# Giving the feature maps and the normalized rows' copies to ScalarE behind the slot's exponential

## The chip, the cores and the metric

The kernel runs on one core of one Trainium2 chip. The metric is the device time of one execution in microseconds (us). A core has TensorE (matmuls; PE in the profile, with PEld for its weight loads), VectorE (DVE), ScalarE (ACT), GpSimd (POOL) and SyncE (SP, which here issues most transfers). Each engine works through its own list of instructions in order, and semaphores make one engine wait for another.

## What is computed

The reference is one transformer block over 2048 rows of width 512, modulated by a condition vector `c`: a layer norm, an attention with a compressive memory (32 heads of width 16, four segments of 512 rows), an output projection, a second layer norm, and a bilinear feed-forward layer of width 1376. What matters here is the attention of one segment:

```python
phi = lambda t: jnp.where(t > 0, t + 1.0, jnp.exp(t))
for s in range(N):                       # 4 segments
    logits = jnp.einsum("bhqd,bhkd->bhqk", qs, ks) * scale + mask
    a_dot = jnp.einsum("bhqk,bhkd->bhqd", _softmax(logits, axis=-1), vs)
    pq = phi(qs)
    a_mem = (pq @ M) / (pq @ z + 1e-6)   # memory of the earlier segments
    o = g * a_mem + (1.0 - g) * a_dot
    pk = phi(ks)
    M = M + pk^T @ vs; z = z + sum(pk)
```

So every segment but the last needs the feature map `phi` of its keys, and every segment but the first that of its queries. The kernel computes `phi(t)` as min(exp(t), 1) + relu(t): a Relu and an Exp on ScalarE and one step on VectorE that joins them.

## The kernel before, in words

The heads are worked in 4 groups (`g`) of 8, for 4 segments (`s`), in halves of 4 heads: 32 units `v`. The main loop (lines 1149 to 1199) takes each unit through five slots. In each slot TensorE's work is given out in this order: the first half of the query-side scores of a later unit (`q_half(u, i, 0)`, PSUM tile `lq0`), whose row maxima VectorE finds in place (tiles `q` and `nm` of the profile); in slot 1 the product of probabilities and values (`av_step`, tile `tb`); in slot 4 the transposes of a finished unit (`t_step`, tile `tr`, read by VectorE as `rd` and `orow`); filler work (`fill`); the second half of the scores (`q_half(u, i, 1)`, tile `lq1`); and the key-side scores (`k_step`, tile `k`), whose exponential ScalarE takes as one operation of 128x1024 (tile `pt`, line 335). `lq0`, `lq1` and `k` have one buffer each: the next matmul into one of them waits until VectorE, or ScalarE, has read it.

The filler `fill_a` (line 974) computes the projections of the next groups: `a_kq` (line 799) runs twelve matmuls for `kps` or `qps` in four steps, copies the result to SBUF (`kf`, `qf`, line 819), takes a first bfloat16 part of it on ScalarE (line 823), and where a feature map is needed gives out `feature` (Relu into `rl`, Exp into `ph`, line 847, each ordered behind the latest exponential given out so far, `lastex`). One step later `rest` (line 826) makes the other two parts, and the list `later` takes up `feature2`, VectorE's joining step. The lists work thus: `flush` gives out all of `later`, after the first half of the scores in each slot and whenever a filler step asks for a PSUM bank (`bank`); `behind` holds closures that the main loop gives out at the end of a slot, behind `k_step` (line 1192); `after_n` goes over to `later` in slot 2; `settle` empties all three, and `a_mem` (the memory step that multiplies `ph` with the memory, tiles `mp`, `up`, `mz`) calls it before it reads `ph`.

In the loop VectorE's instructions are chained in the order in which the program gives them out (`vec.eng = CV`, line 1147). TensorE's are chained too. ScalarE's and GpSimd's are not: the scheduler of the language orders them by when they are ready in its own timeline, and the program's order is the tie-break.

Before the change only two feature maps go through `behind` (`held`, line 854): the keys of groups 2 and 3 of segment 0. In `ln` (line 172) the normalized rows of segments 1 to 3 are transposed, scaled and shifted on ScalarE (`ahf`, line 223), and split at once into a first part on ScalarE (`ahH`, line 233) and a rest on GpSimd (`ahL`, line 234). Slots are called below by the instant of their k matmuls or of their exponential.

Of the kernel before, what the change touches and what calls it, by code (L numbers as in the profile page):

```python
# [8 lines left out]
F32 = mybir.dt.float32  # L9
F32R = mybir.dt.float32r  # L10
BF = mybir.dt.bfloat16
AF = mybir.ActivationFunctionType
# [13 lines left out]
NOSYNC = mybir.DependencyInfo(mybir.DependencyClass.NoSync, mybir.DependencyReason.DATA)  # L26
# [31 lines left out]
def tile_kernel(ctx, tc, x, wq, wk_, wv, wo, beta, w_gate, w_up, w_down, c, w_mod, out):  # L58
    nc = tc.nc
# [19 lines left out]
    def pin(i):  # L79

        if last_pe[0] is not None:
            tc.add_manual_dep(i.ins, last_pe[0].ins.name, NOSYNC, reason="order")
# [4 lines left out]
    def TP(*a):  # L87
        return pe(nc.tensor.transpose(*a))

    CV, CA = Chain(tc, nc.vector), Chain(tc, nc.scalar)  # L90
    vec, act = Switch(nc.vector), Switch(nc.scalar)
# [15 lines left out]
    behind, lastex, after_n, now = [], [None], [], [0]  # L107
# [19 lines left out]
    def bank(name, dt=F32, shape=(P, 512), small=False):  # L127

        flush()
        rest_of()  # L130
        nbank[0] += 1
        tag = btag[nbank[0] % len(btag)]
        if tag == "ms":
            if not small:
                nlast[0] ^= 1
            tag = f"ms{nlast[0] ^ int(small)}"
        return pst(shape, tag, name, dt)
# [34 lines left out]
    def ln(pool, hpool, xt, s, sc, sh, pfx, hb, fast):  # L172

        first = pfx == "a" and s == 0
        V, A = (CV, CA) if first else (vec, act)
        mv = pool.tile([P, 4, 2], F32, tag="mv", name=f"{pfx}mv{s}", bufs=2)
        for t in range(4):
            st = pool.tile([P, 6], F32, tag="st", name=f"{pfx}st{s}_{t}", bufs=2)
            i = V.bn_stats(st, xt[t])
            if not first:  # L180
                pin(i)
            V.bn_aggr(mv[:, t, :], st)
            if not first:
                yield 0.0
        sd = pool.tile([P, 4], F32, tag="sd", name=f"{pfx}sd{s}", bufs=2)
        A.activation(sd, mv[:, :, 1], AF.Ln, bias=epst[:, 0:1])
        y = pool.tile([P, 4], F32, tag="y", name=f"{pfx}y{s}", bufs=2)
        A.activation(y, sd, AF.Exp, scale=-0.5)
        a = pool.tile([P, 4], F32, tag="ya", name=f"{pfx}ya{s}", bufs=2)
        b = pool.tile([P, 4], F32, tag="yb", name=f"{pfx}yb{s}", bufs=2)  # L190
        eng = CV if first else nc.gpsimd
        eng.tensor_mul(a, y, y)
        if first:
            CV.scalar_tensor_tensor(b, mv[:, :, 1], EPS, a, op0=ALU.add, op1=ALU.mult)
        else:
            eng.tensor_scalar(b, mv[:, :, 1], 1.0, EPS, op0=ALU.mult, op1=ALU.add)
            eng.tensor_mul(b, b, a)
        eng.tensor_scalar(b, b, -0.5, 1.5, op0=ALU.mult, op1=ALU.add)
        eng.tensor_mul(y, y, b)
        yield 0.0  # L200
        tps = [bank(f"{pfx}tp{s}_{d}") for d in range(KT)] if first else []
        for t in range(4):
            i = V.tensor_scalar(xt[t], xt[t], mv[:, t, 0:1], y[:, t:t + 1],
                                op0=ALU.subtract, op1=ALU.mult)
            if not first:
                pin(i)
                yield 0.0
            for d, ps in enumerate(tps):
                TP(ps[:, t * P:(t + 1) * P], xt[t][:, d * P:(d + 1) * P], ident)
        if first:  # L210
            yield 0.0
        hH, hL = [], []
        if first:
            hcur[0] = hH, hL
        for d in range(KT):
            if first:
                ps = tps[d]
            else:
                ps = bank(f"{pfx}tp{s}_{d}", small=pfx == "c" and s == 0)
                for t in range(4):  # L220
                    TP(ps[:, t * P:(t + 1) * P], xt[t][:, d * P:(d + 1) * P], ident)
            h = pool.tile([P, L], F32, tag="hf", name=f"{pfx}hf{s}_{d}", bufs=hb[2])
            A.activation(h, ps, AF.Identity, scale=sc[:, d:d + 1], bias=sh[:, d:d + 1])
            hi = hpool.tile([P, L], F32R, tag=hb[0].format(d), name=f"{pfx}hH{s}_{d}", bufs=hb[1])
            lo = hpool.tile([P, L], F32R, tag=hb[0].format(4 + d), name=f"{pfx}hL{s}_{d}", bufs=hb[1])
            if fast:
                if d % 2:
                    A.activation(hi, h, AF.Copy)
                else:
                    V.tensor_copy(hi, h)  # L230
                V.tensor_sub(lo, h, hi.bitcast(F32))
            else:
                act.activation(hi, h, AF.Copy)
                nc.gpsimd.tensor_sub(lo, h, hi.bitcast(F32))
            hH.append(hi)
            hL.append(lo)
            yield 0.45
            if pfx == "a" and not first and d % 2 == 1:
                yield False
        return hH, hL  # L240
# [558 lines left out]
    def a_kq(s, g, nm):  # L799

        hH, hL = hcur[0]
        ph = phs.setdefault((s, g), {})
        if True:
            dst = kd if nm == "k" else qd
            ps = bank(f"{nm}ps{s}_{g}")
            n = 0
            three = ((wH, hH), (wH, hL), (wL, hH)) if s == 0 and g < 2 else ((wH, hH), (wL, hH), (wH, hL))
            terms = [(k, *ab) for k in range(KT) for ab in three]
            if s == 0 and g == 1:
                terms.sort(key=lambda t: t[1] is wL)  # L810
            for k, a, b in terms:
                MM(ps, a[nm, g][:, k, :], b[k], start=n == 0, stop=n == 11)
                n += 1
                if n in (3, 6, 9):
                    yield 0.68
            f = pa.tile([P, L], F32, tag="f", name=f"{nm}f{s}_{g}", bufs=2)
            fast = s == 0 and g == 0
            A, V = (CA, CV) if fast else (act, nc.gpsimd)
            A.activation(f, ps, AF.Copy)
            q3 = pa.tile([P, 3, L], BF, tag="q3", name=f"{nm}3_{s}_{g}", bufs=2)  # L820
            r = pa.tile([P, L], F32, tag="qr", name=f"{nm}r_{s}_{g}", bufs=2)
            i0, i1, i2 = (0, 1, 2) if nm == "k" else (2, 1, 0)
            A.activation(q3[:, i0, :], f, AF.Copy)
            V.tensor_sub(r, f, q3[:, i0, :])

            def rest():
                (CV.tensor_copy if fast else act.copy)(q3[:, i1, :], r)
                V.tensor_sub(q3[:, i2, :], r, q3[:, i1, :])
                nc.sync.dma_start(dst[s][g].rearrange("r p t -> p r t"), q3)

            if fast:
                rest()
            phi = (nm == "k" and s < NSEG - 1) or (nm == "q" and s > 0)
            if phi:
                if fast:
                    yield 0.0
                if nm == "q" and g > 0:
                    yield from drain()
                e = pa.tile([P, L], F32, tag="ph", name=f"ph{nm}{s}_{g}", bufs=3)
                if behind:  # L840
                    settle()
                rl = pa.tile([P, L], F32, tag="rl", name=f"rl{nm}{s}_{g}", bufs=1)
                ph[nm] = e

                def feature():
                    for a, fn in ((rl, AF.Relu), (e, AF.Exp)):
                        i = (CA if fast else act).activation(a, f, fn)
                        if lastex[0] is not None:
                            tc.add_manual_dep(i.ins, lastex[0].ins.name, NOSYNC, reason="order")

                def feature2():
                    pin((CV if fast else vec).scalar_tensor_tensor(e, e, 1.0, rl, op0=ALU.min, op1=ALU.add))

                held = s == 0 and g > 1
                if held:
                    behind.append(lambda: (feature(), (after_n if now[0] == 0 else later).append(feature2)))
                else:
                    feature()
            yield 0.68
            if not fast:  # L860
                rest()
            if phi and not held:
                later.append(feature2)
                if fast:
                    flush()
        nkq[s, g] = nkq.get((s, g), 0) + 1
        if nkq[s, g] == 2:
            done.add((s, g))
# [105 lines left out]
    def fill_a():  # L974
# [5 lines left out]
        for s in range(NSEG):  # L980
            if s > 0:
                hcur[0] = yield from lns
                if s < 3:
                    r = load_mod(2 * s)
            for g in range(2 if s == 0 else 0, NG):
# [163 lines left out]
    for v in range(-2, NQ + 1):  # L1149
        rate[0] = 5.5  # L1150
        on, prev = 0 <= v < NQ, 0 <= v - 1 < NQ
        for slot in range(5):
            i = (slot + 3) % 5
# [450 lines left out]
    for n in range(NU):  # L1604
        p, nm, i = units[n]
# [69 lines left out]
```

## Time and profile before

| | |
|---|---|
| median of 3 runs | 861.65 us (860.18 to 862.78) |
| the profiled execution | 862.23 us, of it 860.5 us from the first instruction to the last |
| VectorE busy | 643.1 us, 75% |
| ScalarE busy | 499.1 us, 58% |
| GpSimd busy | 275.8 us, 32% |

The page gives for each engine its busy time and share of the span. A row of the timeline gives an instruction's start and duration in us, its engine and line, what it writes from what, and in square brackets how long its engine stood idle before it and what ended that wait. Rows of one kind that follow each other are merged (x4). The attention loop runs from about 41 us to about 490 us; the rest is the feed-forward layer.

### The profile page before, as it was taken

What the parts mean: (1) busy time and instruction counts of PE and PEld (TensorE: products, weight loads), DVE (VectorE), ACT (ScalarE), POOL (GpSimd) and SP (SyncE); (2) the same over time, 40 slices, a digit from 0 to 9 for tenths busy, and PEclk for the clock granted to TensorE, in tenths of its full rate; (3) what the DMA queues carried; (4) which work ended last, traced back from release to release, by engine and by line L of the source; (5) the groups of instructions that cost most, each with busy time, mean ns of one, the idle gap of its engine ahead of it and who ended that gap; (6) DMA issues with size and microseconds to landing.
All of it is one profiled execution on the core that took longest, in us unless ns stands there. A gap on an engine that the chain in (4) does not pass through costs nothing.

```text
span 860.5 us, 14421 instructions
## 1 busy us (share of the span) xinstructions
PE 839.1 (98%) x4982; PEld 599.1 (70%) x4982; DVE 643.1 (75%) x1796; ACT 499.1 (58%) x759; POOL 275.8 (32%) x423
## 2 busy tenths in 40 slices
PE   9989999999999999999999999999999999999998
PEld 6756655566665666666665677788888778888886
DVE  6897766887778877687889358989987855446554
ACT  4758766777677786677545626343535546455230
POOL 2756526566545673675424610000000000000000
PEclk9999999999999999999999999999999999999999
DMA  8655433655527463458575447578561576335102
GB/s 269 148 151 158 121 102 88 183 136 167 142 82 197 113 177 100 122 155 245 144 239 166 137 159 247 207 239 324 197 226 50 214 263 212 143 135 183 34 17 98
DMA packets 83929, 139.57 MB, mean 162 GB/s; under 512 B 12721, under 2 KB 46769, under 8 KB 83857
## 3 DMA queue, kind: packets, MB, share of 16 engines
q1 hardware_dynamic: 83568, 138.52, 51.9%
q8 instruction: 39, 0.64, 0.3%
q14 instruction: 34, 0.27, 0.1%
q10 hardware_dynamic: 288, 0.15, 0.1%
HBM read 89.87 MB, written 48.50 MB: 161 GB/s over the span
## 4 chain that ended last, share of the span: by engine, by line
PE 84%; ACT 7%; DVE 6%; issue 1%; POOL 0%; DMA 0%; DVEq 0%; ACTq 0%
PE acc L1351 14%; PE tb L85 8%; PE Xg L1282 7%; PE Xu L1282 7%; PE k L85 6%; PE q L85 6%; PE wops L85 5%; PE vps L85 5%; PE kps L85 4%; PE Yu L1282 4%; PE Yg L1282 4%; DVE q L39 3%; PE qps L85 3%; ACT pt L335 2%; PE Zg L1282 1%; PE Zu L1282 1%
## 5 line engine op out<-in xcount | busy, mean ns | idle before, releaser
L39 DVE CUSTOM_DVE_ANT_0 q<-q,cmask 128x384 f32<-128x384 f32 (+3 forms) x512 | 247.6, 504 | 71.3 <-PE q L85 63.6
L335 ACT ACTIVATE pt<-k 128x1024 f32<-128x1024 f32 x160 | 163.9, 1024 | 76.9 <-PE k L85 75.0
L341 POOL TENSOR_SCALAR_AFFINE_SELECT pt<-pt 128x256 f32<-128x256 f32 (+1 forms) x224 | 98.6, 454 | 152.8 <-ACT pt L335 150.2
L85 PE MATMUL q<-kst,qst 96*128 96x384 bf16 (+3 forms) x512 | 123.0, 302 | 7.6 <-DVE nm L39 6.0
L85 PE MATMUL k<-qst,kst 98*128 98x384 bf16 (+3 forms) x512 | 95.9, 299 | 5.7 <-ACT pt L335 5.2
L1359 DVE TENSOR_TENSOR xa<-xa,acc 128x512 f32<-128x512 f32 x95 | 64.8, 684 | 39.8 <-PE acc L1351 39.3
L85 PEld LDWEIGHTS <-qst 96*128 96x128 bf16 x512 | 44.2, 98 | 59.2 <-issue 44.1
L85 PE MATMUL tb<-pt,v 128*32 128x512 f32 (+3 forms) x1024 | 77.1, 442 | 0.0
L39 DVE DVE_READ_ACCUMULATOR2_ANT nm<- 128x1 f32 x512 | 71.9, 140 | 0.0
L85 PEld LDWEIGHTS <-kst 98*128 98x128 bf16 x512 | 44.5, 97 | 30.2 <-issue 15.2
L1351 PE MATMUL acc<-dH,mH 128*128 128x512 f32 (+1 forms) x152 | 60.3, 397 | 0.0
L1351 PE MATMUL acc<-dL,mH 128*128 128x512 f32 (+1 forms) x152 | 60.1, 395 | 0.0
L1351 PE MATMUL acc<-dH,mL 128*128 128x512 f32 (+1 forms) x152 | 60.0, 394 | 0.0
L85 PEld LDWEIGHTS tb<-pt,v 128*32 128x32 f32 x1024 | 28.8, 110 | 40.1 <-issue 37.3
L367 ACT ACTIVATE tsb<-tb 128x512 f32<-128x512 f32 x32 | 19.1, 596 | 32.5 <-PE tb L85 32.5
L1351 PEld LDWEIGHTS acc<-dL,mH 128*128 128x128 f32 (+1 forms) x152 | 28.6, 188 | 7.0
L1351 PEld LDWEIGHTS acc<-dH,mL 128*128 128x128 f32 (+1 forms) x152 | 28.5, 188 | 7.1 <-DVE mL L1302 0.3
L1351 PEld LDWEIGHTS acc<-dH,mH 128*128 128x128 f32 (+1 forms) x152 | 28.5, 188 | 6.7
L85 PE MATMUL kps<-ahH,wkH 128*128 128x512 f32 x64 | 29.5, 461 | 0.0
L85 PE MATMUL wops<-woH,oH 128*128 128x512 f32 x64 | 28.2, 441 | 0.8 <-ACT oH L530 0.7
L85 PE MATMUL qps<-ahH,wqH 128*128 128x512 f32 x64 | 28.7, 448 | 0.0
L85 PE MATMUL vps<-wvH,ahH 128*128 128x512 f32 x64 | 28.3, 443 | 0.0
(399 smaller groups left out, 2018.4 us busy)
## 6 DMA issues: line engine op xcount, KB each, us to landing
wm<-in_w_mod_dram SPq DMA_DIRECT2D x24, 256.0 KB, 4.9
kd<-k SPq DMA_DIRECT2D x16, 384.0 KB, 2.5
qd<-q SPq DMA_DIRECT2D x16, 384.0 KB, 3.6
kst<-kd SPq DMA_DIRECT2D x32, 192.0 KB, 3.3
qst<-qd SPq DMA_DIRECT2D x32, 192.0 KB, 3.7
x<-in_x_dram SPq DMA_DIRECT2D x16, 256.0 KB, 4.9
kst<-kd SPq DMA_DIRECT2D x32, 128.0 KB, 3.2
qst<-qd SPq DMA_DIRECT2D x32, 128.0 KB, 3.7
```

The costliest lines, as they stand in the source:

```text
L39: i = getattr(self.eng, name)(*a, **k)
L85: return pe(nc.tensor.matmul(*a, **k))
L335: ex = act.activation(pt, kp, AF.Exp, scale=0.25)
L341: sels[u, i] = nc.gpsimd.affine_select(w, w, pattern=[[0, w.shape[1]], [1, P]], compare_op=ALU.is_ge, fill=0.0, base=0, channel_multiplier=-1)
L367: act.activation(tsbs[u], tbs.pop(u), AF.Copy)
L1282: pe(nc.tensor.matmul(ps[0:n], a, b[:, k], start=first and c == 0, stop=last and c == 5, skip_group_check=True))
L1351: pe(nc.tensor.matmul(ps, a[0:m, t * P:(t + 1) * P], b[0:m], start=j == 0, stop=j == n - 1))
L1359: vec.tensor_add(xa, xa, ps)
```

## The change

Three places change. The feature maps of all keys and queries of segments 1 to 3 (20 of them: 8 of keys, 12 of queries) join the two that are given out through `behind`; only those of groups 0 and 1 in segment 0 still go out at once. Their VectorE step then goes into `later` behind them, or into `after_n` where the slot is slot 0. The split of the normalized rows (12 pairs of operations) becomes a closure in `behind` as well, with its ScalarE copy ordered behind the latest exponential. And where the next segment's rows are taken over, `behind` is emptied first.

```diff
@@ in ln
             else:
-                act.activation(hi, h, AF.Copy)
-                nc.gpsimd.tensor_sub(lo, h, hi.bitcast(F32))
+                def parts(hi=hi, lo=lo, h=h):
+                    i = act.activation(hi, h, AF.Copy)
+                    if lastex[0] is not None:
+                        tc.add_manual_dep(i.ins, lastex[0].ins.name, NOSYNC, reason="order")
+                    nc.gpsimd.tensor_sub(lo, h, hi.bitcast(F32))
+
+                behind.append(parts)
@@ in a_kq
-                held = s == 0 and g > 1
+                held = s > 0 or g > 1
                 if held:
                     behind.append(lambda: (feature(), (after_n if now[0] == 0 else later).append(feature2)))
@@ in fill_a
             if s > 0:
                 hcur[0] = yield from lns
+                while behind:
+                    behind.pop(0)()
                 if s < 3:
                     r = load_mod(2 * s)
```

## The prediction

> **What bounds the kernel now.** I read the page's first part, then TensorE's waits inside the attention loop, then the timeline around the feature maps.
>
> ```profile
> span 860.5 us, 14421 instructions
> PE 839.1 (98%) x4982; PEld 599.1 (70%) x4982; DVE 643.1 (75%) x1796; ACT 499.1 (58%) x759; POOL 275.8 (32%) x423
> ```
>
> TensorE is busy for all but 21.4 us of the span. The change takes no matmul away and TensorE's order is chained, so it can only change these idle times and add new ones. The waits of TensorE from 60 to 470 us:
>
> ```profile
> PE k L85 <- ACT pt L335: 5.2, 12, 0.9
> PE q L85 <- DVE nm L39: 3.8, 7, 1.6
> ```
>
> The first row is what the change aims at: a k matmul waits until the exponential has read the slot before. The second is what it can make worse: a q matmul waits until VectorE has taken the maxima out of the same bank. The longest wait of the second kind is 1.6 us, and none of the first kind exceeds 0.9.
>
> **How one slot runs now, and what moves in it.** I take the slot whose k matmuls begin at 271.35:
>
> ```profile
> 271.35 0.60 PE L85 MATMUL k<-qst,kst 98*128 98x384 bf16 x4
> 271.94 0.63 ACT L823 ACTIVATE k<-kf 128x512 bf16<-128x512 f32 x1
> 272.48 0.62 ACT L847 ACTIVATE rlk<-kf 128x512 f32<-128x512 f32 x1
> 273.00 0.62 ACT L847 ACTIVATE phk<-kf 128x512 f32<-128x512 f32 x1
> 273.08 0.25 DVE L39 RECIPROCAL rd<-tr 128x16 f32<-128x16 f32 x1
> 273.52 1.00 ACT L335 ACTIVATE pt<-k 128x1024 f32<-128x1024 f32 x1
> 273.76 0.68 DVE L39 SCALAR_TENSOR_TENSOR phk<-phk,rlk 128x512 f32<-128x512 f32 x1
> 274.36 0.69 DVE L39 BATCH_NORM_STATS2 ast<-x 128x6 f32<-128x512 f32 x1
> 274.43 0.61 ACT L827 CAST k<-kr 128x512 bf16<-128x512 f32 x1
> 274.58 0.60 PE L85 MATMUL k<-qst,kst 98*128 98x256 bf16 x4 [0.34 <-ACT pt L335]
> 275.18 0.67 DVE L39 CUSTOM_DVE_ANT_0 q<-q,cmask 128x512 f32<-128x512 f32 x1
> 275.77 0.14 DVE L39 DVE_READ_ACCUMULATOR2_ANT nm<- 128x1 f32 x1
> 276.46 0.40 PE L85 MATMUL q<-kst,qst 96*128 96x384 bf16 x2
> ```
>
> The scores of k are done at 271.95, but the exponential starts at 273.52: the bfloat16 copy, Relu and Exp stand ahead of it, 1.57 us, and the next k matmuls wait 0.34. **Gain:** behind the change the exponential follows the copy, at 272.48, so it ends 1.04 us earlier and the 0.34 goes.
>
> **Loss:** Relu now starts 0.91 behind the exponential's start (273.52 to 274.43 is that distance), at 273.39, Exp 0.52 later at 273.91, and it ends 0.62 later at 274.53. VectorE's step is given out straight behind the next slot's first reductions, which end here when `rd` starts (273.08). It also passes ahead of `rd` and `orow`, which it followed before. So VectorE stands idle from 273.08 to about 274.56, 1.48 us. Behind it follow, at the distances of the rows, the step itself (0.60, to 275.16), `rd` and `orow` (0.68, to 275.84), the statistics (0.82, to 276.66) and the reduction that began at 275.18, whose maximum is out 0.73 after its start: 277.39 in place of 275.91. The q matmul that uses this bank next stood at 276.46, and without the 0.34 it would come at 276.12; it has to wait to 277.39, that is 1.27. **Net for this slot: +0.93.** What queues behind the waiting instruction is all of VectorE's list: `orow` (which also frees the bank for `up`), the statistics, the maxima; TensorE waits for the maxima and for that bank at the same place, so the two waits are not added.
>
> **The same slot kind where it costs nothing.**
>
> ```profile
> 331.09 0.60 PE L85 MATMUL k<-qst,kst 98*128 98x256 bf16 x4 [0.33 <-ACT pt L335]
> 333.90 0.39 PE L85 MATMUL q<-kst,qst 96*128 96x384 bf16 x2
> 334.33 0.57 DVE L39 CUSTOM_DVE_ANT_0 q<-q,cmask 128x384 f32<-128x384 f32 x1 [1.36 <-PE q L85]
> ```
>
> Here nine matmuls of the values stand between, VectorE sits idle for 1.36 later on, and the q matmul of 333.90 comes late enough. Net -0.33, the stall alone. Seven features lie like these two, in slot 3 before a slot with `rd` and `orow`. Their ends are -0.33 and +0.93 each, -2.3 and +6.5 for all. I take **+0.5 each, +3.5**, nearer to the costly slot, because in most of the seven a statistics, normalizing or memory step stands in VectorE's list as there, and the idle 1.36 is the exception.
>
> Three features lie in slot 2, where no `rd` follows and the two small copies of the maxima shorten VectorE's idle time. The row of one:
>
> ```profile
> 217.04 0.60 PE L85 MATMUL k<-qst,kst 98*128 98x384 bf16 x4 [0.60 <-ACT pt L335]
> ```
>
> At best each gives its stall (0.60 here), at worst it costs what the worked slot does less `rd` and `orow` (0.93 - 0.68 = +0.25). Ends -1.8 and +0.8 for three; I take **0**, between them, since the stall that goes and the wait that comes are alike in size. Two queries given out after the memory step, between slots, I put at +0.2 together, between nothing and the 0.34 of one stall. Six others already ran behind the exponential, or have the value matmuls of slot 1 behind them, and come out at 0.
>
> **Where VectorE was blocked before.** One key map was joined within its own slot, before the second reductions:
>
> ```profile
> 134.12 1.01 ACT L335 ACTIVATE pt<-k 128x1024 f32<-128x1024 f32 x1
> 134.25 1.52 DVE L39 SCALAR_TENSOR_TENSOR phk<-phk,rlk 128x512 f32<-128x512 f32 x1 [2.36 <-ACT phk L847]
> 136.49 0.38 PE L85 MATMUL q<-kst,qst 96*128 96x384 bf16 x2 [1.64 <-DVE nm L39]
> ```
>
> VectorE waited 2.36 us for Exp with reductions queued behind, and TensorE stood 1.64. A slot later the step comes behind the reductions of two banks, and the wait goes: **-1.6**. More hangs on it:
>
> ```profile
> 134.00:137.00 3.00, 1.36 (x8) 0.79 (x7) 2.71 (x6) 2.12 (x4) 3.00 (x4) 1.00 0.03 7
> 137.50:140.50 3.00, 3.00 (x18) 0.79 (x21) 1.59 (x8) 0.86 (x1) 0.41 (x1) 0.50 0.41 137
> 137.91 3.75 PE L85 MATMUL tb<-pt,v 128*32 128x512 f32 x32
> 402.14 2.36 PE L85 MATMUL tb<-pt,v 128*32 128x512 f32 x32
> ```
>
> Behind the stall the granted clock (the figure before the last two of a stretch) fell from 1.00 to 0.50 for at least the three us of the second stretch, and the 32 value matmuls took 3.75 in place of 2.36. So the stall cost another 1.39: **-3.0** in all. The Trainium skill's page "TensorE: Matmul & The Clock Gate" (section "Why this matters for your kernels") wants no idle gaps above about 3 us, and by it neither the old stall nor the new one below would lower the clock; both terms of 1.39 would fall out together. The row differs: 1.64 sufficed, and the measurement decides.
>
> **Where a wait comes anew.** The last query map is given out in a slot 0, so its join goes to slot 2, right before the memory step that reads it:
>
> ```profile
> 403.00 0.73 DVE L39 SCALAR_TENSOR_TENSOR phq<-phq,rlq 128x512 f32<-128x512 f32 x1 [1.66 <-ACT phq L847]
> 404.70 0.38 PE L85 MATMUL q<-kst,qst 96*128 96x256 bf16 x2 [0.20 <-DVE nm L39]
> 405.83 0.63 PE L85 MATMUL up<-MZ,phq 128*128 128x136 f32 x4
> 406.33 0.73 DVE L39 CUSTOM_DVE_ANT_0 q<-q,cmask 128x512 f32<-128x512 f32 x1
> 406.97 0.14 DVE L39 DVE_READ_ACCUMULATOR2_ANT nm<- 128x1 f32 x1
> ```
>
> In slot 2 the order on VectorE is the reduction of 406.33, then the join, and TensorE goes straight to `up`. Without the block at 403.00 all comes about 0.2 earlier (the 0.20 of the second row): the reduction at 406.13, its maximum read from 0.64 later, 406.77, the join 0.60 as in the worked slot, to 407.37, `up` at 407.4 in place of 405.83: **+1.6**, a stall of 1.8. That is longer than the 1.64, so I charge the slow clock too: **+1.4**. Bounds: -0.2 (if `up` finds it done) and +3.0.
>
> **The normalized rows.** Their copies already run behind the exponential:
>
> ```profile
> 76.44 1.02 ACT L335 ACTIVATE pt<-k 128x1024 f32<-128x1024 f32 x1
> 77.35 0.64 ACT L233 ACTIVATE ahH<-ahf 128x512 fp32r<-128x512 f32 x1
> 77.87 0.79 ACT L223 ACTIVATE ahf<-atp,modc 128x512 f32<-128x512 f32 x1
> 78.53 0.63 ACT L827 CAST q<-qr 128x512 bf16<-128x512 f32 x1
> 79.04 1.05 ACT L335 ACTIVATE pt<-k 128x1024 f32<-128x1024 f32 x1
> 80.14 0.59 PE L85 MATMUL k<-qst,kst 98*128 98x512 bf16 x2 [0.56 <-ACT pt L335]
> ```
>
> The copy of line 233 starts right behind the exponential of its slot; what stands ahead of the one of 79.04 are that copy, which keeps its place since its exponential is the one of 76.44, the scaling (L223) and the cast, which do not move. So this part gives **0**, and the 0.56 stays; at best it would give that in each of three segments, -1.7. GpSimd's subtraction follows the copy, and SyncE's list is passed by nothing: the stores behind `rest` stand where they stood, at most one ScalarE operation later, with loads two units ahead.
>
> **The sum:** 3.5 + 0 + 0.2 - 3.0 + 3.0 + 0 = **+3.7 us**. For the profiled execution (862.23, of it 860.5 in the span and 1.7 around it) that is 865.9; it lies 0.6 above the median of the runs, 861.65, so I forecast **865.3**.
>
> **Rivals.**
> - *VectorE's idle time is free* (faster). Against the worked slot stands one map that was already given out like this:
>
> ```profile
> 67.74 0.69 DVE L39 SCALAR_TENSOR_TENSOR phk<-phk,rlk 128x512 f32<-128x512 f32 x1 [0.38 <-ACT phk L847]
> ```
>
> VectorE waited 0.38 there and no wait of TensorE followed. If it is so everywhere, the k stalls go: 5.2 less the 0.56 that has no feature in it is at most -4.6, with -3.0 and +3.0: 857.1. It decides at the next q matmul of the bank: the idle time is free where that comes over 2.8 us (277.39 less 274.56) behind the join's start. For it speaks that VectorE is only 75% busy; against it that the 0.38 followed an exponential that was on time and VectorE's three reductions. Chance 0.15.
> - *Gain and loss cancel.* If the scheduler puts the exponential ahead of the bfloat16 copy too, Relu and Exp come 0.54 earlier, the seven cost 0 and the three give 0.5 each: 3.7 - 3.5 - 1.5 = -1.3, 860.3. In the worked slot the copy went first, at 271.94, just as the scores ended. Chance 0.17.
> - *The order comes out as it was* (the change does not do what it says): 861.7. Against it: the exponential is now an explicit predecessor. Chance 0.05.
> - *The slow clock follows more stalls.* The worked slot gets 1.27; if two such halve the clock, +2.8: 868.1. Nothing in the loop between 0.9 and 1.64 shows where it starts. Chance 0.18.
> - The forecast: 0.45.
>
> **How the numbers follow.** 0.3% is 2.6 us, about what a measurement of this kernel can tell from no change; slower means above 864.2. Of the forecast's 0.45 some 0.08 fall below that. Slower 0.37 + 0.18 = 0.55; same 0.08 + 0.17 + 0.05 = 0.30; faster 0.15. The range takes in all but the faster case and the sums of several high ends: 859.8 to 869.0.
>
> **What would show it.** Right: the exponentials of slots 2 and 3 start 0.54 behind their scores; TensorE's waits for `pt` fall to about 1; those for `nm` in slots after a feature rise from 3.8 to some 7, less the 1.64 at 134.85; joins wait on VectorE for Exp in most of the slots; `up` waits for the last join near 407; the clock falls there and not near 137. Wrong: waits for `nm` stay as they are, or the joins stand behind `rd` and `orow`.

## The result, and the profile after

The changed kernel takes 862.46 us in the median of 18 runs (861.84 to 864.39), the kernel before beside it 860.82 (859.96 to 863.12): ratio 1.0019, with a 95% interval of 1.0011 to 1.0026. That is 1.6 us slower, less than the 0.3% that was called no change; forecast were 865.3 and +3.7. The two profiled executions, 862.65 and 862.23 us, differ by only 0.4; the one of before holds a fall of the clock, of which more below.

The page of the changed kernel: the engines run the same instructions, and TensorE's idle time in the span rose from 21.4 to 23.4 us (860.9 less 837.5), while its busy time fell from 839.1 to 837.5.

```profile
span 860.9 us, 14421 instructions
PE 837.5 (97%) x4982; PEld 598.6 (70%) x4982; DVE 639.5 (74%) x1796; ACT 499.1 (58%) x759; POOL 272.4 (32%) x423
```

TensorE's waits between 60 and 470 us of the changed kernel (engine, tile and line, what it waited for; us in total, times, longest):

```profile
PE q L85 <- DVE nm L39: 2.7, 8, 0.6
PE up L85 <- DVE phq L39: 1.7, 1, 1.7
PE up L85 <- DVE orow L39: 1.5, 2, 1.2
PE mz L85 <- DVE orow L39: 1.1, 1, 1.1
PE k L85 <- ACT pt L340: 1.1, 3, 0.6
PE mp L88 <- DVE orow L39: 0.7, 1, 0.7
```

The fifth row is what the change was for: the k matmuls wait 1.1 us in place of 5.2. The rest of the list is what it cost. The `nm` row lost its 1.6 at the blocked map, but three rows for `orow` are new, 1.5 + 1.1 + 0.7 = 3.3, and one for `phq`, the last join. Five more rows that before does not have, of 0.2 to 0.5 each and 1.6 in all (`tr`, `atp`, `kps`, `up` behind `pkr`, and one `q` behind a transfer), are left out here. VectorE's own waits from 60 to 410 us say why:

```profile
DVE phk L39 <- ACT phk L852: 8.9, 9, 1.5
DVE phq L39 <- ACT phq L852: 5.9, 6, 1.3
```

The same view of the kernel before:

```profile
DVE phk L39 <- ACT phk L847: 5.1, 4, 2.4
DVE phq L39 <- ACT phq L847: 1.7, 1, 1.7
```

VectorE now idles 14.8 us in front of joins that wait for Exp, 15 times; before it was 6.8 in 5 cases. The worked slot in the timeline of the changed kernel:

```profile
269.55 0.60 PE L85 MATMUL k<-qst,kst 98*128 98x384 bf16 x4
270.14 0.63 ACT L828 ACTIVATE k<-kf 128x512 bf16<-128x512 f32 x1
270.68 1.01 ACT L340 ACTIVATE pt<-k 128x1024 f32<-128x1024 f32 x1
271.58 0.62 ACT L852 ACTIVATE rlk<-kf 128x512 f32<-128x512 f32 x1
272.10 0.62 ACT L852 ACTIVATE phk<-kf 128x512 f32<-128x512 f32 x1
272.27 0.60 PE L85 MATMUL k<-qst,kst 98*128 98x256 bf16 x4
272.75 0.69 DVE L39 SCALAR_TENSOR_TENSOR phk<-phk,rlk 128x512 f32<-128x512 f32 x1 [1.34 <-ACT phk L852]
273.36 0.25 DVE L39 RECIPROCAL rd<-tr 128x16 f32<-128x16 f32 x1
273.70 0.43 DVE L39 TENSOR_TENSOR orow<-tr,rd 128x256 f32<-128x256 f32 x1
274.27 0.70 PE L85 MATMUL up<-MZ,phq 128*128 128x136 f32 x4 [1.18 <-DVE orow L39]
275.45 0.14 DVE L39 DVE_READ_ACCUMULATOR2_ANT nm<- 128x1 f32 x1
275.65 0.38 PE L85 MATMUL q<-kst,qst 96*128 96x384 bf16 x2
```

Read it from top to bottom: the exponential starts 0.53 behind the scores instead of 1.57, and the next k matmuls (272.27) wait for nothing. VectorE idles 1.34 before the join (forecast 1.48), `rd` and `orow` come behind it, and TensorE stands 1.18 (forecast 1.27). But it stands at `up`, whose bank `orow` frees, and not at the q matmul, where the forecast put the wait; the q matmul at 275.65 then waits for nothing.

The last query map in the changed kernel, and the clock behind it (per stretch: length, busy time of PE, PEld, DVE, ACT, POOL with counts, granted clock, DMA share, GB/s):

```profile
404.67 0.73 DVE L39 CUSTOM_DVE_ANT_0 q<-q,cmask 128x512 f32<-128x512 f32 x1
405.32 0.69 DVE L39 SCALAR_TENSOR_TENSOR phq<-phq,rlq 128x512 f32<-128x512 f32 x1
406.06 0.73 PE L85 MATMUL up<-MZ,phq 128*128 128x136 f32 x4 [1.65 <-DVE phq L39]
```

```profile
137.50:140.50 3.00, 2.94 (x20) 1.97 (x20) 2.20 (x9) 2.71 (x5) 0.41 (x1) 1.00 0.38 131
404.40:406.10 1.70, 0.05 (x2) 0.04 (x1) 1.60 (x5) 0.85 (x1) 1.14 (x2) 1.00 0.29 98
406.10:409.50 3.40, 3.40 (x24) 2.73 (x25) 1.25 (x5) 1.85 (x3) 0.17 (x1) 1.00 0.22 76
```

`up` waited 1.65, right where it was forecast. The clock behind it stayed at 1.00 all the same, and also behind the map that was blocked before (first row; 0.50 in the profile of before).

How much of the time each step took is read by comparing, slot by slot, the instant at which the k matmuls end in both traces; the table gives how the distance changes over each step's slots.

| step of the sum | forecast | the two traces |
|---|---|---|
| seven maps of slot 3 | +3.5 | +0.13 +0.42 +1.12 +0.81 +1.23 -0.52 +0.21 = +3.4 |
| three maps of slot 2 | 0 | +0.31 -0.68 -0.05 = -0.4 |
| two after the memory step, and others | +0.2 | +0.4 |
| the blocked key map: stall, slow clock | -1.6, -1.4 | -1.8, -1.85 |
| the last query map: stall, slow clock | +1.6, +1.4 | +1.4, none |
| sum in the loop | +3.7 | +1.1 |

The loop also began 0.79 earlier in the trace after. The traces of experiments 1 to 8 have their first k matmuls 0 to 1 us earlier than the one of before as well, whatever their edit (those of 9 and 10 1.2 to 1.5 earlier), so this is not put down to the change.

The -1.85 is not all clock. Two other traces have no fall in the loop and differ in the feature maps alone: that of the row part alone (experiment 6) and the second one of the changed kernel (experiment 7). Compared in the same way, they give -1.77 and -0.25 at the blocked map, so the map without its fall is worth -2.0, and the fall costs some 1.6. The other steps are +3.4 for slot 3, -0.4 for slot 2, +1.4 for the last map and -0.1 for the rest: +2.3 in the loop, without any fall.

### The profile page after: what moved, and what is told of

It reads as the page before. It is cut to its first block, busy times and chain, and to the rows that moved or that the text cites. A ratio compares the mean times of both kernels' runs of the same rounds, so it can differ in the third digit from the quotient of the medians.

```text
span 860.9 us, 14421 instructions
## 1 busy us (share of the span) xinstructions
PE 837.5 (97%) x4982; PEld 598.6 (70%) x4982; DVE 639.5 (74%) x1796; ACT 499.1 (58%) x759; POOL 272.4 (32%) x423
## 4 chain that ended last, share of the span: by engine, by line
PE 83%; DVE 9%; ACT 4%; DMA 1%; issue 1%; POOL 1%; SPq 0%; DVEq 0%
PE acc L1358 14%; PE tb L85 8%; PE Xu L1289 7%; PE Xg L1289 7%; PE q L85 6%; PE k L85 6%; PE vps L85 5%; PE wops L85 5%; DVE q L39 4%; PE Yu L1289 4%; PE Yg L1289 4%; PE kps L85 4%; PE qps L85 3%; ACT pt L340 2%; PE Zg L1289 1%; PE Zu L1289 1%
```

## Experiments

The theory: the step is one for VectorE's order. A join given out straight behind the first reductions waits for an Exp that now ends later, and all of VectorE's list waits with it; that and the last map are the loss, the blocked map is the gain. The rivals: that the loss comes from the moved ScalarE operations themselves, wherever the join stands; that the row part takes a share; and that the slow clock moved from one stall to the other, and with it the time. An execution's record gives its mean granted clock. One with a fall of the clock in the loop shows 0.998 or less; 0.999 can come from the last 2 us, behind the last matmul, as in the profile of the changed kernel (0.54 from 859 us on). Where it matters the two sorts are given apart, since their share differs from series to series. The executions of before that stand beside these runs are 53 without a fall (medians of the three groups 860.21, 860.41 and 860.33) and 14 with one (862.02, 862.29, 862.22).

**1. The blocked key map alone.** Before, with `held` true for one more map:

```diff
-                held = s == 0 and g > 1
+                held = s == 0 and g > 1 or (nm, s, g) == ("k", 1, 1)
```

> The kernel before with one feature map alone moved, the keys of segment 1, group 1, whose join blocked VectorE for 2.36 us. Theory (the 1.64 us stall goes in every execution, the slow clock only in those that had it): -1.6 to -2.0 us against the kernel before in the median, and no execution some 2 us above the others. Rival (as the prediction summed it, stall and slow clock both belong to the typical execution): -3.0. Rival (the idle time turns up again later): 0.

858.03 us, ratio 0.9977 (0.9967 to 0.9986); no fall of the clock in 9 executions. Against 860.21 that is -2.2 without any fall, somewhat more than the -1.6 to -2.0 expected. The timeline:

```profile
134.66 0.39 PE L85 MATMUL q<-kst,qst 96*128 96x384 bf16 x2
135.13 1.19 DVE L39 SCALAR_TENSOR_TENSOR phk<-phk,rlk 128x512 f32<-128x512 f32 x1 [1.10 <-ACT phk L847]
```

VectorE still waits 1.10 for this Exp, but the q matmul of 134.66 already has its maxima and does not wait. This one map of the 20, moved alone, makes the kernel faster.

**2. The seven maps of slot 3 alone.**

```diff
-                held = s == 0 and g > 1
+                held = s == 0 and g > 1 or (nm, s, g) in (("k", 1, 0), ("q", 1, 1), ("k", 1, 3), ("k", 2, 0), ("k", 2, 2), ("q", 3, 0), ("q", 3, 2))
```

> The kernel before with the seven feature maps of slot 3 alone moved. Theory (VectorE stands idle some 1.3 us in front of each join, with rd, orow and the maxima queued behind it): +3.4 us against the kernel before, with waits of TensorE for orow and nm. Rival (VectorE's idle time is free, only the waits for the exponential go): -2 us. Rival (the sum was too high because these seven cost less than 0.5 each): 0 to +1.5.

865.46 us, ratio 1.0056 (1.0044 to 1.0069); 864.32 without a fall (2 executions), +4.1 against 860.21. Its waits:

```profile
PE q L85 <- DVE nm L39: 5.0, 11, 1.6
PE k L85 <- ACT pt L335: 3.0, 6, 0.8
PE up L85 <- DVE orow L39: 1.2, 1, 1.2
PE mz L85 <- DVE orow L39: 1.1, 1, 1.1
PE mp L88 <- DVE orow L39: 1.0, 1, 1.0
```

The k waits fall by 2.2, and 1.2 + 1.1 + 1.0 of `orow` and 1.2 more of `nm` come in. These rows add up to +2.3 only; between the k matmuls of this trace and of before, both with a fall, the loop lost 3.6. The rest does not show as a wait that the view lists. The +4.1 rests on two executions, but both ways the term of +3.5 stands.

**3. The three maps of slot 2 alone.**

```diff
-                held = s == 0 and g > 1
+                held = s == 0 and g > 1 or (nm, s, g) in (("k", 1, 2), ("q", 2, 0), ("q", 2, 3))
```

> The kernel before with the three feature maps of slot 2 alone moved. Prediction: 0, between -1.8 and +0.8. Theory (from the changed kernel's trace: the k waits of 0.85, 0.60 and 0.50 go, VectorE's idle time in front of the join is 0.9 at most and no rd and orow stand behind it): -0.4 us. Rival (they are the gain that the sum missed): -1.5 to -2.

860.40 us, ratio 1.0000 (0.9991 to 1.0008); without a fall 860.00 against 860.41. A gain of 0.4 at most, and none that can be told from nothing.

**4. The last query map alone.**

```diff
-                held = s == 0 and g > 1
+                held = s == 0 and g > 1 or (nm, s, g) == ("q", 3, 3)
```

> The kernel before with the last query map (segment 3, group 3) alone moved. Theory: the wait of up for the join, 1.65 us, less the 0.3 of waits that go, +1.4 us in executions whose clock stays up; now two stalls of over 1.6 us stand in one execution, so more of the executions than before should show a clock below 0.999, each about 1.6 us longer. Rival (the prediction's price, the new stall always halves the clock): +3.0 in every execution.

863.68 us, ratio 1.0031 (1.0019 to 1.0042). Two executions without a fall: 861.50, +1.2 against 860.33; nine with one: 863.76. Three of the nine, 864.86 to 865.59, have a mean clock of 0.996, which is room for two falls. Its profiled execution is one of the nine:

```profile
404.75 0.73 PE L85 MATMUL up<-MZ,phq 128*128 128x136 f32 x4 [1.65 <-DVE phq L39]
```

```profile
402.00:405.00 3.00, 1.35 (x11) 0.66 (x8) 2.17 (x7) 1.81 (x3) 2.10 (x2) 1.00 0.56 190
405.60:408.80 3.20, 3.20 (x13) 1.91 (x12) 0.76 (x2) 0.91 (x2) 0.00 (x0) 0.50 0.00 1
```

Here is the fall to 0.50 that the changed kernel's profile does not have, behind the same wait of 1.65. So the mechanism of the forecast exists at `up`, but not in every execution. In this same execution the old stall, 1.64 at 135.48, was followed by a clock of 1.00 (137.0 to 140.4).

**5. The changed kernel with the last query map at once.**

```diff
-                held = s > 0 or g > 1
+                held = (s > 0 or g > 1) and (s, g) != (3, 3)
```

> The changed kernel with the last query map (segment 3, group 3) given out at once again, as before the change. Theory (the wait of up for the join costs its 1.65 us and nothing else, the clock stays up in most executions): 1.4 us faster than the changed kernel, so about +0.2 us against the kernel before. Rival (as the prediction priced it, the stall also halves the clock most times, 1.4 more): 2.8 us or more faster than the changed kernel, -1.2 against the kernel before.

861.00 us, ratio 1.0008 (0.9999 to 1.0017); no fall in 11 executions, +0.8 against 860.21 where the changed kernel had +2.0 in its first series (862.4 against about 860.4). So the last map is worth 1.2 here too, and without it, and without its clock falls, little is left of the loss.

**6. The row part alone, and the feature maps alone.** The first is the changed kernel with the first of these edits, the second with the other (`def parts` to `behind.append(parts)` taken out):

```diff
-                held = s > 0 or g > 1
+                held = s == 0 and g > 1
```

```diff
-                behind.append(parts)
+                act.activation(hi, h, AF.Copy)
+                nc.gpsimd.tensor_sub(lo, h, hi.bitcast(F32))
```

> The kernel before with the change of the normalized rows' first parts alone, the feature maps as before. Prediction: 0, since those copies ran behind the exponential anyway. Rival, from the trace of the changed kernel (waits of 0.23 for up behind pkr and of 0.28 for kps behind GpSimd's ahL in segment 3, that the kernel before has not): +0.3 to +0.7 us.

> The changed kernel without its part on the normalized rows. Theory (the waits for ahL and pkr in segment 3 come from that part together with the moved maps): 0.3 to 0.7 us faster than the changed kernel, the 0.28 wait of kps for ahL gone. Prediction: no difference.

The rows alone: 860.57 us, ratio 1.0006 (0.9997 to 1.0015), no difference that can be told from nothing. The feature maps alone: 862.59, ratio 1.0026 (1.0016 to 1.0036), as the whole change. The row part is worth 0, as forecast. The small waits of `kps` and of `up` behind `pkr` that the changed kernel has are there with the feature maps alone and not with the rows alone, so they do not come from the rows.

**7. The changed kernel again,** beside 8 and 9 on the same chip.

> The changed kernel once more, as the measure for the two below on one chip: +1.6 us against the kernel before, and in most executions no fall of the clock at the wait of up.

864.13 us, ratio 1.0035 (1.0022 to 1.0047): two executions without a fall, 862.99, and three with one, 864.55. In the first series 16 of 18 had none. The same code, and its median moves by 1.7, in part with that share.

**8. The join behind `rd` and `orow`.** The changed kernel with a list `joins` that takes up `feature2` in place of `later` and is emptied behind `t_step` (and by `settle`, which is not shown):

```diff
-                    behind.append(lambda: (feature(), (after_n if now[0] == 0 else later).append(feature2)))
+                    behind.append(lambda: (feature(), (after_n if now[0] == 0 else joins).append(feature2)))
...
+            later.extend(joins)
+            joins.clear()
+            flush()
             fill(share[slot], slot < 4)
```

> The changed kernel with the joins given out behind rd and orow in slot 4 instead of ahead of them. Theory (VectorE's wait in front of the join is the cost, and rd and orow fill 0.68 of it): the waits of TensorE for orow go, those for nm shrink by up to 0.68 in each of six slots, 2 to 3.5 us faster than the changed kernel, -0.4 to -2 against the kernel before. Rival (the order of rd and orow does not matter, VectorE's total work does): 0 to -0.5 against the changed kernel.

860.19 us, ratio 0.9992 (0.9983 to 1.0001); without a fall 860.00 against the 862.99 of the changed kernel: -3.0, with only two executions behind the 862.99; the two profiled executions, without a fall, have spans of 861.1 and 857.9, -3.2. The worked slot:

```profile
270.05 0.25 DVE L39 RECIPROCAL rd<-tr 128x16 f32<-128x16 f32 x1
271.53 0.69 DVE L39 SCALAR_TENSOR_TENSOR phk<-phk,rlk 128x512 f32<-128x512 f32 x1 [0.71 <-ACT phk L854]
271.71 0.68 PE L85 MATMUL up<-MZ,phq 128*128 128x136 f32 x4
273.75 0.38 PE L85 MATMUL q<-kst,qst 96*128 96x384 bf16 x2 [0.66 <-DVE nm L39]
```

ScalarE's order is the changed kernel's; only VectorE's is not. Here `up` no longer waits, and 0.66 is left at the q matmul. So the rival that the moved ScalarE operations cost the time by themselves falls.

**9. The join a whole slot later.** The same list, emptied at the end of the next slot, behind its second reductions:

```diff
-                    behind.append(lambda: (feature(), (after_n if now[0] == 0 else later).append(feature2)))
+                    behind.append(lambda: (feature(), joins.append(feature2)))
...
+            ripe = joins[:]
+            joins.clear()
             while behind:
                 behind.pop(0)()
...
+            for join in ripe:
+                join()
```

> The changed kernel with each join given out at the end of the next slot, behind its second reductions and the key-side scores, so that Exp is long done. Theory (all that the change costs is VectorE's waiting for Exp, and the memory step waiting for the join): no wait of VectorE for ph, the waits for orow and nm behind a feature go, the gains stay: 4 to 7 us faster than the changed kernel, -3 to -5 against the kernel before. Rival (VectorE is full there and the 0.6 of a join delays the maxima wherever it stands): 0 to -2 against the changed kernel.

856.22 us, ratio 0.9949 (0.9935 to 0.9962). VectorE's waits from 60 to 410 us shrink from 14.8 to one row:

```profile
DVE phk L39 <- ACT phk L854: 1.5, 2, 1.1
```

This is the change's gain without most of its loss: -4.2 against 860.41, and -6.8 against the changed kernel, as the profiled spans have it too (861.1 and 854.3). What is left of the loss is mainly 1.0 us of `up` waiting for the last join.

**10. The best of them.** Experiment 9 with the rows as before (the second edit of 6) and the last query map at once:

```diff
-                held = s > 0 or g > 1
+                held = (s > 0 or g > 1) and (s, g) != (3, 3)
```

> The joins at the end of the next slot, the last query map at once as in the kernel before, and the normalized rows as before. Theory: the wait of up (1.0 us with the joins at the slot's end) and the row part go, 0.5 to 1.2 us faster than the kernel with the joins at the slot's end alone, -4.8 to -5.5 against the kernel before. Rival (the last map at once brings back the block of VectorE and gains nothing): -4.3.

855.21 us, ratio 0.9939 (0.9926 to 0.9951), faster than both kernels. Its waits from 60 to 470 us:

```profile
PE q L85 <- DVE nm L39: 3.4, 8, 1.0
PE k L85 <- ACT pt L337: 1.3, 4, 0.6
PE up L85 <- DVE orow L39: 0.3, 1, 0.3
```

The k waits are nearly as short as in the changed kernel (1.1), of `orow` 0.3 is left, and no wait for `phq` appears.

## Why the prediction was off in size

- **What bounds it, and the mechanism: right.** The exponential came 0.53 behind the scores, the k waits fell to 1.1, the joins stood ahead of `rd` and `orow` and idled in 15 cases, and experiments 8 and 9 show that this order is what costs: moving the join alone gives 3.0 and 6.8 back.
- **The seven maps of slot 3, +3.5: right in sum.** +3.4 between the traces, +4.1 alone. But +0.5 each was a choice between two ends, -0.33 and +0.93, and the single maps go beyond both, from -0.52 to +1.23 (the worked slot), so that the sum came out so close has some luck in it. The wait came at `up`, `mz` and `mp` rather than at the q matmul; the forecast had named the bank but put the price on the wrong instruction. All `nm` and `orow` waits together are 2.7 + 3.3 = 6.0, where it said 7 less 1.64.
- **The rows, 0: right** within what was measured (+0.3, not clear of nothing).
- **The slow clock: the step that failed in its mechanism.** The forecast read 0.50 behind the old stall in one trace and charged it as a part of every execution: -1.4 there, and "so I charge the slow clock too: +1.4" at `up`. Of 67 executions of before 14 have a fall, of 23 of the changed kernel 5. So the typical execution of either has none, and neither term belongs into its sum. That the two cancelled there is luck. They did not cancel in the base: the profiled execution on which the sum was laid, 862.23, held a fall that costs some 1.8 (862.02 against 860.21), the median of three that corrected it is 861.65, and a typical execution is near 860.4. Of the 2.8 us between 865.3 and 862.46 some 1.2 (861.65 less 860.4) is this base. The Trainium skill's page "TensorE: Matmul & The Clock Gate" (section "What's actually happening") gives the window as 3413 ns and says that it is free-running and does not reset when a kernel starts. Falls that last 3.41 us in only some executions agree with that, but no run here shows the phase.
- **The two stalls and the maps of slot 2: the terms mis-sized in +3.7.** With the clock the blocked map stood in the sum at -3.0 and the last one at +3.0, together 0. Alone they measured -2.2 and +1.2, between the traces without a fall -2.0 and +1.4: together -0.6 to -1.0. The maps of slot 2, put at 0, gave -0.4 alone and in the traces, though alone that is not clear of nothing. That is 1.0 to 1.4 of the 1.7 by which the change without falls (+2.0 in the first series) missed +3.7; "two after the memory step, and others" came out at -0.1 instead of +0.2. Why the blocked map gave more than its wait of 1.64 is not shown. In the series of experiment 7 the change is +2.6; each of these differences is uncertain by some 0.8 us, and the parts measured alone (4.1 - 0.4 - 2.2 + 1.2 = 2.7) need not add up exactly. That the first series shows 1.6 and not 2.0 fits with the falls: four of its 18 executions of before lie above 862.4, where executions with a fall lie, but no clock is on record for them.

Of the rivals, "idle time is free" is shown wrong by experiments 2 and 8, and "the order comes out as it was" by the trace. "Gain and loss cancel" gave -1.3 us, and its reason failed as well: the exponential did not pass the bfloat16 copy. "The slow clock follows more stalls" did not happen: in the kernels whose longest wait in the loop is 1.2 us or less (1, 5, 9, 10) none of 30 executions has a fall, 11 of them (experiment 5) with waits of 1.18 and 1.12.

## What to carry to other kernels

Where an engine works in order, moving one engine's operation later moves its consumer's place too: give the consumer out where its input is sure to be there, or it holds up everything behind it, here up to 1.5 us of idle time per map and some +3.5 us over seven maps. One slot later it still idled 1.5 us in all, and the kernel was 6.8 us faster than the changed one. Look among many equal edits for the one that carries the gain, and for the last one before a reader that waits. Before a single trace's disturbance is put into a sum, ask in how many executions it occurs, and lay the sum on an execution without it.

## What the runs showed of the hardware

Behind a TensorE wait of 1.63 to 1.65 us in the loop the granted clock fell to 0.50 in some executions and stayed at 1.00 in others; in the traces of before and of experiments 2 and 4 the fall lasted 3.41 us. Executions with a fall are 14 of 67 of before and 5 of 23 of the changed kernel. All kernels with one such wait together have 31 of 139, the one with both stalls (experiment 4) 9 of 11, and those where no wait in the loop exceeds 1.2 have none of 30. Where between 1.2 and 1.63 it begins, and why experiment 4 has it so often, is not settled.

The join of 0.69 us in the worked slot took 1.66 in experiment 9:

```profile
268.95 1.17 POOL L835 TENSOR_TENSOR k<-kr,k 128x512 bf16<-128x512 f32 x1 [0.57 <-ACT k L834]
269.00 1.66 DVE L39 SCALAR_TENSOR_TENSOR phk<-phk,rlk 128x512 f32<-128x512 f32 x1
```

GpSimd's subtraction began 0.05 earlier and ended at 270.12; the join ended 0.54 after that, at 270.66. The Trainium skill's page "SBUF — State Buffer" (section "SBUF: two separate sides") says that a VectorE operation with two SBUF inputs and a GpSimd operation that reads SBUF exclude each other, whichever starts first keeping the ports to its end. The rows agree, and so does the old blocked join of 1.52 us, which ended at 135.77, 0.55 after a subtraction of GpSimd that ran from 134.05 to 135.22; but no run here took the GpSimd operation away.
